# Loading q with four tokens to a partition, in two DMAs a unit, in a retention-plus-WaveMLP kernel

## The chip, the cores and the metric

The kernel runs on one core of one Trainium2 chip. The metric is device time in microseconds (us) of one execution; for the kernel before, three runs gave a median of 165.22 us (165.19 to 165.68). A core has five engines that work side by side and meet only at semaphores: TensorE (PE, with PEld for its weight loads), VectorE (DVE), ScalarE (ACT), GpSimd (POOL) and SyncE (SP). SP and ACT start DMAs from queues of their own (SPq, ACTq); POOL starts the few DMAs that change the type on the way.

## The reference

```python
state = gamma * state + k[t] outer v[t]          # per batch and head, 768 tokens, D = 64
y[t]  = scale * (q[t] @ state)                   # 4 batches, 8 heads
x     = heads of y side by side                  # (4, 768, 512)
theta = x @ w_theta
y     = w_tok_r @ (x*cos(theta)) + w_tok_i @ (x*sin(theta))     # over tokens
u     = x + y
out   = u + max(u @ w_ch, 0)
```

The first half is linear attention with one decay per head; the second mixes tokens and channels. The token mixing needs all tokens of a batch, so the second half of a batch follows its first half.

## The kernel before

The attention is cut into 24 units: 4 batches x 3 blocks of 256 tokens x 2 groups of 4 heads. A unit n loads its q, k and v (`Lq.n`, `Lk.n`, `Lv.n`, lines 154 to 170), each one DMA of 256 KB: partition p gets the tokens 2p and 2p+1 of four heads, so each DMA is 512 rows of 512 bytes. The raw q and k share a pool of 16 buffers (`kqf`), v has 9 (`vf`).

The unit's raw k is cast to bf16 (`ck`, line 295), its q is cast (`cq`) or multiplied with a decay table `qsc` (`cqs`, line 302), its v multiplied with a table `vsc` (`cv`, line 308). TensorE transposes k and q (`Tk`, `Tq`, line 316) into PSUM, `E.n` copies the result to `kqT` (or a DMA transpose `Dk.n` does both). `A.n` multiplies k with q within blocks of 128 tokens, `m.n` applies the causal mask, `ST.n` sums k times v into the state, `I.n` and `Y.n` make the output, which `XA`/`XB` copy out. The two blocks of 128 tokens of a unit are called c = 0 and 1; the head pairs j = 0 and 1. The second half works on 24 tiles of 128 tokens: `Hh` (theta), `CN` (sine and cosine), `z`, `M` (token mixing, the bulk of TensorE's work), `u`, `O` and `f`, and `SO` stores.

The order of everything is a list written out by hand, `ORDER` (lines 22 to 86). Each token is a step with the engine or queue that does it: `Lk.4.a` is the load of k of unit 4, started by ACT; `.s` is SP, `.v` DVE, `.p` POOL. Every engine runs its own steps strictly in the order of the list. The start of the list, its loads and the steps beside them, reads (with others left out):

```
const2 Lv.0.s const1 ... Lk.0.a const3 ... Lq.0.s Lv.1.s ... constA const4 Lq.1.a const9 Lk.1.s
... const8 ck.0.p Tk.0 ck.1.a cqs.0.v cv.0.v Tq.0 E.0.v Lq.4.a ST.0 Lk.4.a cqs.1.p Tq.1 Lq.2.s ... Lk.2.s
... Lv.2.s ... Lq.3.s ... Lk.3.s ... ck.3.p ... cqs.3.p Tq.3 Lv.3.s ... ck.4.p Lv.4.s Lk.5.s Lq.5.s Lv.5.s
Lq.6.s Lk.6.s Lv.6.s Lq.7.s E.3.a ...
```

Three more things set when a load starts. First, SP's and ACT's DMAs take eight semaphores in turn, in the order of the program and across both queues (`DMAHW0` to `DMAHW7` in the list of instructions); a DMA waits, on the engine that starts it, until the DMA before it on the same semaphore has landed. So a DMA waits for the eighth one before it, on whichever queue that is. Second, a buffer must be free. Third, the queue is in order: what stands behind a waiting DMA waits too.

Constants are made at the start. `const2` (lines 203 to 219) has POOL write token numbers `posn` and the eight logarithms `lg`, and DVE multiply them to `arg`; `const1` has DVE write `zero`, with which TensorE does filler products `Z` (line 278) while it has nothing else; `const3` has ACT make `qsc` and `vsc` from `arg`; `const5` is the causal mask, `constA` (line 221) POOL's `pos` and `lgp`, from which ACT makes the table `qx` in eight steps (`const9` and `const8`, line 233).

Of the kernel before, what the change touches and what calls it, by code (L numbers as in the profile page):

```python
# [15 lines left out]
FT = mybir.dt.float32  # L16
BF = mybir.dt.bfloat16
AF = mybir.ActivationFunctionType
# [70 lines left out]
def _bcast_last(ap: bass.AP, n: int) -> bass.AP:  # L89
    return bass.AP(tensor=ap.tensor, offset=ap.offset, ap=list(ap.ap) + [[0, n]])  # L90


def _bcast_mid(ap: bass.AP, n: int) -> bass.AP:
    pat = list(ap.ap)
    return bass.AP(tensor=ap.tensor, offset=ap.offset,
                   ap=[pat[0], [0, n]] + pat[1:])
# [3 lines left out]
def kernel(  # L100
# [13 lines left out]
    nc = tc.nc  # L114
    B, H, S, D = q.shape
    dm = H * D
    P = 128
    nT = S // P
    nD = dm // P
    nI = nT // 2  # L120
    HU = H // 2
    scale = 1.0 / math.sqrt(D)
    gammas = [1.0 - 2.0 ** (-5.0 - h) for h in range(H)]
# [3 lines left out]
    const = ctx.enter_context(tc.tile_pool(name="const", bufs=1))  # L127
    io = ctx.enter_context(tc.tile_pool(name="io", bufs=2))
    work = ctx.enter_context(tc.tile_pool(name="work", bufs=3))
# [3 lines left out]
    engines = {"p": nc.gpsimd, "v": nc.vector, "a": nc.scalar}  # L133

    def copy(e, dst, src):
        if e == "a":
            nc.scalar.copy(dst, src)  # L137
        else:
            engines[e].tensor_copy(dst, src)  # L139
# [4 lines left out]
    def unit(n):  # L144
        i, h = divmod(n, 2)
        b, i = divmod(i, nI)
        return b, i, h


    raw = {}  # L150

    queues = {"s": nc.sync, "a": nc.scalar}

    def load_unit(name, src, n, e):
        b, i, h = unit(n)
        t = io.tile([P, HU, 2, D], FT, name="vf" if name == "vf" else "kqf", bufs=9 if name == "vf" else 16)
        queues[e].dma_start(  # L157
            out=t.rearrange("p h a d -> p h (a d)"),
            in_=src[b, h * HU:(h + 1) * HU, i * 2 * P:(i + 1) * 2 * P, :].rearrange(
                "h (p a) d -> p h (a d)", a=2))  # L160
        raw[name, n] = t

    def Lk(n, e):
        load_unit("kf", k, n, e)

    def Lq(n, e):
        load_unit("qf", q, n, e)

    def Lv(n, e):
        load_unit("vf", v, n, e)  # L170
# [17 lines left out]
    K = {}  # L188
# [14 lines left out]
    def const2():  # L203
        posn = const.tile([P, nI, 2], FT, name="posn")
        nc.gpsimd.iota(posn, pattern=[[2 * P, nI], [1, 2]], base=1, channel_multiplier=2,
                       allow_small_or_imprecise_dtypes=True)
        lg = const.tile([P, H], FT, name="lg")
        for h in range(H):
            nc.gpsimd.memset(lg[:, h:h + 1], math.log(gammas[h]))
        K["lscale"] = const.tile([P, 1], FT, name="lscale")  # L210
        nc.gpsimd.memset(K["lscale"], math.log(scale))
        K["halfpi"] = const.tile([P, 1], FT, name="halfpi")
        nc.gpsimd.memset(K["halfpi"], math.pi / 2.0)
        K["zerob"] = const.tile([P, 1], FT, name="zerob")
        nc.gpsimd.memset(K["zerob"], 0.0)
        arg = const.tile([P, nI * 2, H], FT, name="arg")
        nc.vector.tensor_mul(arg, _bcast_last(posn.rearrange("p i a -> p (i a)"), H),
                             _bcast_mid(lg, nI * 2))
        K["arg"] = arg

    def constA():
        pos = big.tile([P, S], FT, name="pos", tag="z")
        nc.gpsimd.iota(pos, pattern=[[1, S]], base=1, channel_multiplier=0,
                       allow_small_or_imprecise_dtypes=True)
        K["pos"] = pos
        K["lgp"] = const.tile([P, H // 2], FT, name="lgp")
        for h in range(H):
            nc.gpsimd.memset(K["lgp"][(h % 2) * D:(h % 2 + 1) * D, h // 2:h // 2 + 1],
                             math.log(gammas[h]))
# [4 lines left out]
                                 bias=K["lscale"], scale=K["lgp"][:, x:x + 1])  # L234

    def const3():
        K["qsc"] = const.tile([P, nI, 2, H], FT, name="qsc")
        K["vsc"] = const.tile([P, nI, 2, H], FT, name="vsc")
        for t, bias, sc in ((K["qsc"], K["lscale"], 1.0), (K["vsc"], K["zerob"], -1.0)):
            nc.scalar.activation(t.rearrange("p i a h -> p (i a) h"), K["arg"], AF.Exp,  # L240
                                 bias=bias, scale=sc)
        K["qx"] = const.tile([P, H // 2, S], FT, name="qx")

# [13 lines left out]
        K["ident"] = ident  # L257

    def const5():
        mask = const.tile([P, 2, 2, D], BF, name="mask")  # L260
        nc.gpsimd.memset(mask, 1.0)
        for c in range(2):
            rows = slice(c * D, (c + 1) * D)
            for a in range(2):
                nc.gpsimd.affine_select(
                    out=mask[rows, a], in_=mask[rows, a], compare_op=ALU.is_ge, fill=0.0,
                    base=-a, pattern=[[1, 2], [2, D]], channel_multiplier=-2)
        K["mask"] = mask

    def const6(e):  # L270
# [10 lines left out]
    st = {}  # L281

    def kqb_of(n):
        if ("kqb", n) not in st:
            st["kqb", n] = work.tile([P, 2, dm], BF, name="kqb", bufs=5)
        return st["kqb", n]

    def by_token(ap):
        return ap.rearrange("p h a d -> p a h d")

    def in_blocks(ap):
        return ap.rearrange("p (a h d) -> p a h d", a=2, h=HU)

    def ck(n, e):
        copy(e, in_blocks(kqb_of(n)[:, 0]), by_token(raw["kf", n]))

    def cq(n, e):
        copy(e, in_blocks(kqb_of(n)[:, 1]), by_token(raw["qf", n]))

    def cqs(n, e):  # L300
        _, i, h = unit(n)
        engines[e].tensor_mul(in_blocks(kqb_of(n)[:, 1]), by_token(raw["qf", n]),  # L302
                              _bcast_last(K["qsc"][:, i, :, h * HU:(h + 1) * HU], D))

    def cv(n, e):
        _, i, h = unit(n)
# [16 lines left out]
        kq_half(n, 1)  # L323

    def E(n, e):
        kqT = work.tile([P, 2, 2, 2, P], BF, name="kqT", bufs=4)
        copy(e, kqT.rearrange("p w a j t -> p (w a j) t"), st["kq_ps", n])
        st["kqT", n] = kqT

    def Dk(n):  # L330
        kqT = work.tile([P, 2, 2, 2, P], BF, name="kqT", bufs=4)
        nc.sync.dma_start_transpose(
            out=kqT.rearrange("p w a j t -> p (w a j) t"),
            in_=st["kqb", n].rearrange("p w d -> p (w d)"))
        st["kqT", n] = kqT

    def A(n):
        kqT = st["kqT", n]
        at_ps = psum.tile([P, 2, 2, 2, P], FT, name="at_ps", tag="at", bufs=1)
        for j in range(2):  # L340
            for a in range(2):
                for c in range(2):
                    cols = slice(c * D, (c + 1) * D)
                    for g in range(2):
                        rows = slice(g * D, (g + 1) * D)
                        nc.tensor.matmul(at_ps[cols, g, j, a, :],  # L346
                                         kqT[rows, 0, a, j, cols],
                                         kqT[rows, 1, :, j, cols],
                                         start=(j == 0 and a == 0),
                                         stop=(j == 1 and a == 1), skip_group_check=True)  # L350
        st["at_ps", n] = at_ps
# [8 lines left out]
    def R_of(n):  # L360
        if ("R", n) not in st:
            st["R", n] = [bank("r_ps", f"R{c}") for c in range(2)]
        return st["R", n]
# [33 lines left out]
    def sbd_of(n):  # L397
        return K["sbd"][n % 2][n // 2 % 2]
# [7 lines left out]
    def I(n):  # L406
        _, i, h = unit(n)
        r = R_of(n + 1)
        for c in range(0 if i else 1, 2):
            for j in range(2):  # L410
                nc.tensor.matmul(r[c][:, j * P:(j + 1) * P], sbd_of(n)[:, c, j, :],  # L411
                                 st["kqT", n][:, 1, :, j, c * D:(c + 1) * D],
                                 start=(j == 0), stop=False, skip_group_check=True)

    def Y(n):
# [13 lines left out]
    def out_of(n, c):  # L429
        h, C = n % 2, n // 2 * 2 + c  # L430
        if ("xT", C) not in st:
            st["xT", C] = work.tile([P, 4, P], BF, name="xT", bufs=4)
        return (st["xT", C][:, 2 * h:2 * h + 2].rearrange("p j (t a) -> p j t a", a=2),
                st["R", n + 1][c][:, :2 * P].rearrange("p (j a t) -> p j t a", j=2, a=2))

    def XB(n, c, e):
        copy(e, *out_of(n, c))

    def XA(n, c):
        _, i, h = unit(n)  # L440
        nc.vector.tensor_mul(
            *out_of(n, c),
            K["qx"][:, 2 * h:2 * h + 2, (2 * i + c) * P:(2 * i + c + 1) * P].rearrange(
                "p j (t a) -> p j t a", a=2))

    def x_of(C):
        b, c = divmod(C, nT)
# [199 lines left out]
```

## Time and profile before

| | |
|---|---|
| median of three runs | 165.22 us |
| span of the profiled execution, first to last instruction | 163.6 us |
| around that span, against the median | 1.6 us |
| instructions | 4928 |
| PE, DVE, ACT, POOL busy | 155.2, 114.0, 78.9, 74.3 us |
| DMA packets | 69062, 34.93 MB |
| granted TensorE clock | 1.000 |

The span is cut into what each engine did; "busy" is time in which an instruction of the engine ran. Busy PE time counts pipelined products from end to end, so a PE that is 95% busy is not one at its peak, but a stretch in which it is busy all through has no wait of note. The DMA share is the time of packets, summed over 16 DMA engines and divided by 16 and the stretch; packets overlap, so it goes above 1. A row of the timeline gives start, duration, engine, line and operation; what stands in brackets is how long the engine idled before and what released it.

### The profile page before, as it was taken

The numbers are of one execution on the slowest core, as the hardware profiler recorded it, in microseconds if no ns is written. First come the engines' busy times: TensorE is split into PE (matmuls) and PEld (weight loads), VectorE is DVE, ScalarE is ACT, GpSimd is POOL, SyncE is SP. The second block draws the span as 40 slices with busy tenths as digits, with TensorE's granted clock in tenths as the row PEclk, the third lists the DMA queues.
The fourth block names the chain that finished last, engine by engine and source line by source line (L and its number), as shares of the span: only waits on it lengthen the run. The fifth ranks groups of instructions, "written<-read, shape, count | busy, mean of one in ns | idle before, by whom it ended". The sixth has DMA issues, their size and how long they took to land.

```text
span 163.6 us, 4928 instructions
## 1 busy us (share of the span) xinstructions
PE 155.2 (95%) x2034; PEld 87.2 (53%) x2034; DVE 114.0 (70%) x215; ACT 78.9 (48%) x140; POOL 74.3 (45%) x107
## 2 busy tenths in 40 slices
PE   5996889999999999999999999999999999999992
PEld 1453655656666655654554565554545554444561
DVE  3388687887994895984879894887867760345372
ACT  4976697974658255773343726732341616000020
POOL 7557389075034552730227599950469204600000
PEclk9999999999999999999999999999999999999999
DMA  3999999999999999999999999999897548515546
GB/s 115 297 290 255 268 283 236 275 220 286 220 162 232 223 291 139 338 203 270 324 263 198 134 268 221 242 193 298 125 245 136 103 92 227 160 64 128 129 164 224
DMA packets 69062, 34.93 MB, mean 214 GB/s; under 512 B 26416, under 2 KB 66096, under 8 KB 69040
## 3 DMA queue, kind: packets, MB, share of 16 engines
q1 hardware_dynamic: 56032, 23.73, 69.4%
q10 hardware_dynamic: 10320, 7.47, 17.7%
q0 software_dynamic: 2688, 3.41, 12.1%
q8 instruction: 16, 0.26, 0.7%
q14 instruction: 6, 0.05, 0.1%
HBM read 25.69 MB, written 6.29 MB: 196 GB/s over the span
## 4 chain that ended last, share of the span: by engine, by line
PE 76%; DMA 8%; ACT 5%; POOL 3%; issue 2%; SPq 2%; DVE 1%; POOLq 0%; ACTq 0%
PE y_ps L509 36%; PE o_ps L536 11%; PE th_ps L469 10%; DMA kqf<-in_k_dram 8%; PE r_ps L423 3%; ACT qx L233 3%; PE w_ps L491 3%; PE at_ps L346 3%; PE r_ps L411 2%; PE kq_ps L316 2%; SPq L157 2%; PE y_ps L561 2%; ACT cs L476 1%; PE x_ps L455 1%; PE r_ps L373 1%
## 5 line engine op out<-in xcount | busy, mean ns | idle before, releaser
L509 PE MATMUL y_ps<-z,wtr 128*128 128x512 bf16 x138 | 52.4, 380 | 0.0
L509 PE MATMUL y_ps<-z,wti 128*128 128x512 bf16 x138 | 52.3, 379 | 0.0
L483 POOL TENSOR_TENSOR z<-cs,x_sb 128x1024 bf16<-128x1024 bf16 x12 | 25.5, 2136 | 17.9 <-ACT cs L476 10.0
L355 DVE TENSOR_TENSOR at<-at_ps,mask 128x1024 bf16<-128x1024 f32 x24 | 29.2, 1216 | 0.2
L469 PE MATMUL th_ps<-wth,xT 128*128 128x512 bf16 x96 | 24.5, 379 | 0.5 <-ACT cs L476 0.4
L516 DVE TENSOR_TENSOR u<-y_ps,x_sb 128x512 bf16<-128x512 f32 x23 | 15.8, 688 | 12.7 <-PE y_ps L509 12.6
L542 DVE SCALAR_TENSOR_TENSOR ot<-o_ps,u 128x512 f32<-128x512 f32 x22 | 15.1, 688 | 12.5 <-PE o_ps L536 12.4
L308 POOL TENSOR_TENSOR vb<-vf,vsc 128x512 bf16<-128x512 f32 x15 | 15.6, 1041 | 17.3 <-DMA vf<-in_v_dram 16.9
L476 ACT ACTIVATE cs<-th_ps,zerob 128x512 bf16<-128x512 f32 x24 | 16.4, 685 | 13.3 <-PE th_ps L469 8.8
L536 PE MATMUL o_ps<-wch,uT 128*128 128x512 bf16 x88 | 22.6, 379 | 0.0
L476 ACT ACTIVATE cs<-th_ps,halfpi 128x512 bf16<-128x512 f32 x24 | 16.3, 686 | 11.5 <-issue 5.4
L509 PEld LDWEIGHTS <-wtr 128*128 128x128 bf16 x138 | 13.5, 98 | 12.7
L509 PEld LDWEIGHTS <-wti 128*128 128x128 bf16 x138 | 13.5, 98 | 12.0 <-issue 0.2
L139 POOL CAST sbd<-s 64x256 bf16<-64x256 f32 (+1 forms) x21 | 10.1, 481 | 20.8 <-DVE s L391 17.7
L137 ACT COPY kqT<-kq_ps 128x1024 bf16<-128x1024 bf16 x12 | 12.1, 1012 | 11.9 <-PE kq_ps L316 11.9
L469 PEld LDWEIGHTS <-xT 128*128 128x128 bf16 x96 | 8.8, 98 | 8.7 <-issue 0.5
L137 ACT CAST kqb<-kqf 128x512 bf16<-128x512 f32 x16 | 9.6, 620 | 6.9 <-DMA kqf<-in_k_dram 6.3
L536 PEld LDWEIGHTS <-uT 128*128 128x128 bf16 x88 | 8.1, 98 | 8.3
L278 PE MATMUL zz<-zero 128*128 128x512 bf16 x30 | 10.3, 476 | 1.9 <-DVE zero L192 1.9
L423 PE MATMUL r_ps<-at,vb 64*64 64x128 bf16 x384 | 9.9, 221 | 1.6 <-DVE at L355 1.6
L316 PE MATMUL kq_ps<-ident,kqb 128*128 128x128 bf16 x120 | 11.2, 220 | 0.3 <-POOL kqb L302 0.3
L139 POOL CAST kqb<-kqf 128x512 bf16<-128x512 f32 x12 | 7.2, 612 | 8.5 <-DMA kqf<-in_k_dram 8.4
(80 smaller groups left out, 208.7 us busy)
## 6 DMA issues: line engine op xcount, KB each, us to landing
vf<-in_v_dram SPq DMA_DIRECT2D x20, 256.0 KB, 5.9
kqf<-in_k_dram SPq DMA_DIRECT2D x19, 256.0 KB, 5.3
kqf<-in_q_dram SPq DMA_DIRECT2D x17, 256.0 KB, 5.8
out_dram<-ot ACTq DMA_DIRECT2D x12, 256.0 KB, 2.7
out_dram<-ot SPq DMA_DIRECT2D x11, 256.0 KB, 2.9
kqf<-in_q_dram ACTq DMA_DIRECT2D x7, 256.0 KB, 5.2
kqf<-in_k_dram ACTq DMA_DIRECT2D x5, 256.0 KB, 6.6
vf<-in_v_dram ACTq DMA_DIRECT2D x4, 256.0 KB, 5.8
```

What stands on the lines that cost most here:

```text
L137: nc.scalar.copy(dst, src)
L139: engines[e].tensor_copy(dst, src)
L308: engines[e].tensor_mul(in_blocks(vb), by_token(raw["vf", n]), _bcast_last(K["vsc"][:, i, :, h * HU:(h + 1) * HU], D))
L355: nc.vector.tensor_mul(at.rearrange("p g j a t -> p (g j) (a t)"), st["at_ps", n].rearrange("p g j a t -> p (g j) (a t)"), _bcast_mid(K["m ...
L423: nc.tensor.matmul(st["R", n + 1][c][g * D:(g + 1) * D, j * P:(j + 1) * P], st["vb", n][rows, lo:lo + D], st["at", n][rows, g, j, a, :], s ...
L469: nc.tensor.matmul(th_ps, st["xT", C][:, j, :], K["wth"][:, j, :], start=(j == 0), stop=(j == 3))
L476: nc.scalar.activation(st["cs", C][:, w, :], st["th_ps", C], AF.Sin, bias=K["zerob" if w else "halfpi"], scale=1.0)
L483: engines[e].tensor_mul(st["z", b][:, c], st["cs", C], _bcast_mid(x_of(C), 2))
L509: nc.tensor.matmul(st["y", t], K["wT"][r][:, s0, t0 * P:(t0 + 1) * P], st["z", b][:, s0, r, :], start=(done == 0 and r == 0), stop=(done = ...
L516: nc.vector.tensor_add(st["u", t], st["y", t], st["x", b][:, t0, :])
L536: nc.tensor.matmul(o_ps, st["uT", t][:, j, :], K["wch"][:, j, :], start=(j == 0), stop=(j == nD - 1))
L542: nc.vector.scalar_tensor_tensor(st["ot", t], st["o", t], 0.0, st["u", t], ALU.max, ALU.add)
```

## The change

Only the load of q and what depends on its layout is touched; `ORDER` is the same. A unit's q now comes in two DMAs, j = 0 and 1, each for two heads: partition j*64 + p gets the tokens 4p to 4p+3 of the heads 2j and 2j+1. A DMA writes 64 partitions with 2 rows of 1024 bytes each, 128 KB. As k and v stay as they were, q's tokens now come in another order than k's, and the tables for q and the views that read it follow:

```diff
     def Lq(n, e):
-        load_unit("qf", q, n, e)
+        b, i, h = unit(n)
+        t = io.tile([P, 2, 4, D], FT, name="kqf", bufs=16)
+        for j in range(2):
+            h0 = h * HU + 2 * j
+            queues[e].dma_start(
+                out=t[j * D:(j + 1) * D].rearrange("p g a d -> p g (a d)"),
+                in_=q[b, h0:h0 + 2, i * 2 * P:(i + 1) * 2 * P, :].rearrange(
+                    "g (p a) d -> p g (a d)", a=4))
+        raw["qf", n] = t
...
     def const2():
...
+        posq = const.tile([P, nI, 4], FT, name="posq")
+        lgq = const.tile([P, H // 2], FT, name="lgq")
+        for j in range(2):
+            rows = slice(j * D, (j + 1) * D)
+            nc.gpsimd.iota(posq[rows], pattern=[[2 * P, nI], [1, 4]], base=1,
+                           channel_multiplier=4, allow_small_or_imprecise_dtypes=True)
+            for x in range(H // 2):
+                head = x // 2 * HU + 2 * j + x % 2
+                nc.gpsimd.memset(lgq[rows, x:x + 1], math.log(gammas[head]))
         lg = const.tile([P, H], FT, name="lg")
...
         K["arg"] = arg
+        argq = const.tile([P, nI * 4, H // 2], FT, name="argq")
+        nc.vector.tensor_mul(argq, _bcast_last(posq.rearrange("p i a -> p (i a)"), H // 2),
+                             _bcast_mid(lgq, nI * 4))
+        K["argq"] = argq
...
-        mask = const.tile([P, 2, 2, D], BF, name="mask")
+        mask = const.tile([P, 2, 4, D // 2], BF, name="mask")
...
-                    base=-a, pattern=[[1, 2], [2, D]], channel_multiplier=-2)
+                    base=-a, pattern=[[1, 4], [4, D // 2]], channel_multiplier=-2)
...
-        copy(e, in_blocks(kqb_of(n)[:, 1]), by_token(raw["qf", n]))
+        copy(e, in_blocks(kqb_of(n)[:, 1], 4), by_token(raw["qf", n]))
...
+    def qT(n, rows, j, c):
+        lo = j * D + c * (D // 2)
+        return st["kqT", n][rows, 1, :, lo:lo + D // 2]
...
-                                         kqT[rows, 0, a, j, cols],
-                                         kqT[rows, 1, :, j, cols],
+                                         kqT[rows, 0, 2 * a + j, cols],
+                                         qT(n, rows, j, c),
...
-                                 st["kqT", n][:, 1, :, j, c * D:(c + 1) * D],
+                                 qT(n, slice(0, P), j, c),
...
-        return (st["xT", C][:, 2 * h:2 * h + 2].rearrange("p j (t a) -> p j t a", a=2),
-                st["R", n + 1][c][:, :2 * P].rearrange("p (j a t) -> p j t a", j=2, a=2))
+        return (st["xT", C][:, 2 * h:2 * h + 2].rearrange("p j (t a) -> p j t a", a=4),
+                st["R", n + 1][c][:, :2 * P].rearrange("p (j a t) -> p j t a", j=2, a=4))
```

`const3` takes `argq` for `qsc`; `XA` and `cqs` follow with a = 4. All products, copies and scalings of a unit keep their number and their sizes.

More of the change, by code (lines that the diff above doesn't have):

```diff
@@ L236, in const3 @@
     def const3():
-        K["qsc"] = const.tile([P, nI, 2, H], FT, name="qsc")
+        K["qsc"] = const.tile([P, nI, 4, H // 2], FT, name="qsc")
         K["vsc"] = const.tile([P, nI, 2, H], FT, name="vsc")
-        for t, bias, sc in ((K["qsc"], K["lscale"], 1.0), (K["vsc"], K["zerob"], -1.0)):
-            nc.scalar.activation(t.rearrange("p i a h -> p (i a) h"), K["arg"], AF.Exp,
+        for t, arg, bias, sc in ((K["qsc"], K["argq"], K["lscale"], 1.0),
+                                 (K["vsc"], K["arg"], K["zerob"], -1.0)):
+            nc.scalar.activation(t.rearrange("p i a h -> p (i a) h"), arg, AF.Exp,
                                  bias=bias, scale=sc)
@@ L289, in by_token, with in_blocks @@
         return ap.rearrange("p h a d -> p a h d")
-    def in_blocks(ap):
-        return ap.rearrange("p (a h d) -> p a h d", a=2, h=HU)
+    def in_blocks(ap, a=2):
+        return ap.rearrange("p (a h d) -> p a h d", a=a, d=D)
     def ck(n, e):
@@ L297, in cq @@
     def cq(n, e):
-        copy(e, in_blocks(kqb_of(n)[:, 1]), by_token(raw["qf", n]))
+        copy(e, in_blocks(kqb_of(n)[:, 1], 4), by_token(raw["qf", n]))
     def cqs(n, e):
         _, i, h = unit(n)
-        engines[e].tensor_mul(in_blocks(kqb_of(n)[:, 1]), by_token(raw["qf", n]),
-                              _bcast_last(K["qsc"][:, i, :, h * HU:(h + 1) * HU], D))
+        engines[e].tensor_mul(in_blocks(kqb_of(n)[:, 1], 4), by_token(raw["qf", n]),
+                              _bcast_last(K["qsc"][:, i, :, 2 * h:2 * h + 2], D))
     def cv(n, e):
@@ L325, in E @@
     def E(n, e):
-        kqT = work.tile([P, 2, 2, 2, P], BF, name="kqT", bufs=4)
-        copy(e, kqT.rearrange("p w a j t -> p (w a j) t"), st["kq_ps", n])
+        kqT = work.tile([P, 2, 4, P], BF, name="kqT", bufs=4)
+        copy(e, kqT.rearrange("p w x t -> p (w x) t"), st["kq_ps", n])
         st["kqT", n] = kqT
     def Dk(n):
-        kqT = work.tile([P, 2, 2, 2, P], BF, name="kqT", bufs=4)
+        kqT = work.tile([P, 2, 4, P], BF, name="kqT", bufs=4)
         nc.sync.dma_start_transpose(
-            out=kqT.rearrange("p w a j t -> p (w a j) t"),
+            out=kqT.rearrange("p w x t -> p (w x) t"),
             in_=st["kqb", n].rearrange("p w d -> p (w d)"))
         st["kqT", n] = kqT
+    def qT(n, rows, j, c):
+        lo = j * D + c * (D // 2)
+        return st["kqT", n][rows, 1, :, lo:lo + D // 2]
     def A(n):
@@ L443, in XA @@
             K["qx"][:, 2 * h:2 * h + 2, (2 * i + c) * P:(2 * i + c + 1) * P].rearrange(
-                "p j (t a) -> p j t a", a=2))
+                "p j (t a) -> p j t a", a=4))
     def x_of(C):
```

## The prediction

> **What bounds the kernel now.** I read the page first, then the table by stretches of time, then the chain of work that ended last, and last the queues of SP, ACT and POOL over the first 30 us.
>
> ```profile
> span 163.6 us, 4928 instructions
> PE 155.2 (95%) x2034; PEld 87.2 (53%) x2034; DVE 114.0 (70%) x215; ACT 78.9 (48%) x140; POOL 74.3 (45%) x107
> ...
> 5.00:10.00 5.00, 4.73 (x58) 2.45 (x57) 3.24 (x7) 4.46 (x8) 3.00 (x6) 1.00 1.22 290
> 10.00:15.00 5.00, 3.89 (x102) 2.43 (x100) 3.85 (x8) 4.03 (x7) 3.65 (x5) 1.00 1.23 290
> 30.00:40.00 10.00, 9.99 (x129) 6.28 (x132) 8.28 (x18) 6.76 (x12) 5.55 (x6) 1.00 1.16 258
> 140.00:150.00 10.00, 10.00 (x51) 4.71 (x49) 3.93 (x7) 0.00 (x0) 1.54 (x1) 1.00 0.48 144
> ```
>
> The stretch rows give busy PE, PEld, DVE, ACT, POOL, then the clock, the DMA share and GB/s. From 30 us to 150 us PE never waits (9.99 and 10.00 of 10 us): there the time is PE's work, and no load can shorten it. Before that PE is short of input (3.89 of 5 us), and DMA runs flat out: 290 GB/s, so 262144 bytes / 290 GB/s = 0.90 us for each load of 256 KB. So the end is the moment at which PE gets its unbroken work, plus a fixed amount. The chain shows that moment:
>
> ```profile
> 3.95 4.90 ACT qx L233 x8
> 8.85 0.43 ACT kqb L137
> 9.32 6.61 DMA kqf<-in_k_dram
> 15.94 0.37 SPq L157
> 16.36 0.51 SPq L157
> 16.91 0.51 SPq L157
> 17.46 1.81 SPq L157
> 19.31 5.96 DMA kqf<-in_k_dram
> 25.37 1.14 ACT kqb L137 x2
> 26.51 1.17 ACT cs L476 x2
> 27.72 1.02 PE th_ps L469 x4
> ```
>
> ACT makes `qx` in eight steps, casts k of unit 1 (`ck.1.a`), and only then starts `Lq.4.a` and `Lk.4.a` (9.32). `Lk.4` lands at 15.93, and at 15.94 SP starts `Lk.5`: that is the wait for the eighth DMA before. Behind it in SP's queue come `Lq.5`, `Lv.5`, `Lq.6`, `Lk.6` (19.31), which lands at 25.3, lets `ck.6.a` run, and at 27.72 `Hh.3` starts the unbroken stretch. The semaphores, not the bytes alone, tie SP's queue to ACT's.
>
> **The change part by part.**
>
> *The start on POOL and DVE.* `const2` gets two iotas and eight memsets of 64x1 more, ahead of all that POOL does, and DVE one product more.
>
> ```profile
> 0.91 0.15 POOL L205 IOTA posn<- 128x6 f32 x1 [0.39 <-POOLq L631]
> 1.02 0.32 POOL L209 MEMSET lg<- 128x1 f32 x8
> 3.68 1.07 POOL L228 MEMSET lgp<- 64x1 f32 x8
> 1.38 0.21 DVE L217 TENSOR_TENSOR arg<-posn,lg 128x48 f32<-128x48 f32 x1 [1.38 <-POOL lscale L211]
> 1.59 0.27 DVE L192 MEMSET zero<- 128x256 uint32 x1
> 8.85 0.43 ACTq L157 DMA_DIRECT2D kqf<-in_q_dram  x1
> ```
>
> Two iotas are 2 x 0.15 = 0.30 us. Eight memsets took 0.32 us as `lg` and 1.07 us as `lgp`, so the addition is 0.62 to 1.37; I take 1.2, since `lgp` has the same 64x1 form. On DVE the product adds 0.21, so `zero`, the fillers behind it and the table load that ACT starts after `argq` come 1.4 later. `qx` needs `lgp` and moves from 3.95 to 5.15; with it `ck.1.a` from 8.85 to 10.05, and the loads behind it: `Lq.4` half 0 at 10.05, half 1 at 10.5, `Lk.4` at 10.95 (0.43 each to start, and a gap).
>
> *The semaphores.* Every q now takes two of the eight. Which DMA waits for which follows from the lists of instructions; SP's list of the changed kernel reads, from the third load of q on:
>
> ```
> 9  L173 DMACopy kqf<-in_q_dram 64x2x256 [waits DMAHW7_49]    Lq.3, half 0
> 10 L173 DMACopy kqf<-in_q_dram 64x2x256 [waits DMAHW0_49]    Lq.3, half 1
> 11 L159 DMACopy kqf<-in_k_dram 128x4x128 [waits DMAHW1_49]   Lk.3
> 12 L159 DMACopy vf<-in_v_dram 128x4x128 [waits DMAHW2_49]    Lv.3
> ```
>
> The DMAs before these on semaphores 0, 1 and 2 are ACT's `Lq.4` half 0, half 1 and `Lk.4`. In the kernel before, SP meets these three only at `Lv.4` and `Lk.5`; unit 3 waited for loads of unit 1, long landed, and SP started its k at 8.38. Now SP stands before unit 3 until ACT is through with `qx` and its load has landed.
>
> ```profile
> 8.38 0.51 SPq L157 DMA_DIRECT2D kqf<-in_k_dram  x1
> DMA to landing us min/median/max: 3.7/5.4/12.7
> kqf<-in_q_dram SPq DMA_DIRECT2D x1, 256.0 KB, 4.5
> kqf<-in_k_dram SPq DMA_DIRECT2D x1, 256.0 KB, 5.0
> 13.54 0.62 POOL L139 CAST kqb<-kqf 128x512 bf16<-128x512 f32 x1
> 14.12 1.05 POOL L302 TENSOR_TENSOR kqb<-kqf,qsc 128x512 bf16<-128x512 f32 x1
> 16.35 0.39 PE L316 MATMUL kq_ps<-ident,kqb 128*128 128x128 bf16 x4
> 24.11 0.40 ACT L137 CAST sbd<-s 64x256 bf16<-64x256 f32 x1
> 25.37 1.14 ACT L137 CAST kqb<-kqf 128x512 bf16<-128x512 f32 x2 [0.85 <-DMA kqf<-in_k_dram]
> ```
>
> The shortest landing of a q or k load is 3.7 us, the two loads of unit 3 took 4.5 and 5.0 in a full pipe. While SP waits, the pipe runs empty, so I take 3.7 for `Lq.4`: half 0 lands at 10.05 + 3.7 = 13.75, half 1 at 14.2, `Lk.4` at 14.7. SP starts `Lq.3` half 1 at 13.75, `Lk.3` at 14.25, `Lv.3` at 14.95. With 4.0 us (3.7 to 5.0) `Lk.3` lands at 18.25, where it landed at 8.38 + 5.0 = 13.4. POOL casts k and scales q of unit 3 from 18.25 instead of 13.54, done at 18.25 + 0.58 + 1.05 = 19.9; PE's transposes of that q, at 16.35 before, come at 19.9, 3.55 late, and PE, in order, holds back all behind them.
>
> What is late next: the steps from there to `ck.6.a` are a chain of compute (unit 3 to 5), and ACT was free at 25.37 - 0.85 = 24.52, waiting for `Lk.6`. With 3.55 more it is free at 28.07. Is `Lk.6` there by then? It now waits for `Lv.3`: 14.95 + 5.4 = 20.35, plus the 5.96 of the chain = 26.3. It is. So `ck.6.a` starts 28.07 - 25.37 = 2.7 later, and PE's unbroken work with it. The delay of 1.4 of the fillers and of units 0 to 2 runs beside this wait and does not add. With the small ends (0.62 and 3.7 us) the same steps give 1.8; with the large ones (1.37 and 5.0 for both landings) 5.1, so I keep +1.8 to +5.1 and take +2.7, near the small end because the pipe is empty.
>
> *The packets.* A load of q has 256 packets of 1024 bytes in place of 512 of 512.
>
> ```profile
> q1 hardware_dynamic: 56032, 23.73, 69.4%
> q10 hardware_dynamic: 10320, 7.47, 17.7%
> out_dram<-ot SPq DMA_DIRECT2D x11, 256.0 KB, 2.9
> out_dram<-oh SPq DMA_DIRECT2D x1, 128.0 KB, 2.0
> ```
>
> Queue 1 spent 0.694 x 16 x 163.6 / 56032 = 32.4 ns on a packet of 424 bytes, queue 10 44.9 ns on one of 724. The line through both gives 36 ns at 512 bytes and 57 at 1024, so a q takes 16 engines 0.91 us instead of 1.15, a gain of 0.24. By `Lk.6` that is 7 x 0.24 = 1.7 us of pipe; but the path above waits for semaphores and not for the pipe, so it gains nothing there. No row shows a load into 64 partitions. At the other end each half could take as long as a whole load, 0.90 us, and a q 0.90 more; I take an unchanged 0.90 for a q.
>
> [...]
>
> *Issue slots.* SP starts 17 more DMAs, ACT 7.
>
> ```profile
> L157 SPq DMA_DIRECT2D kqf<-in_q_dram x17: 367/557/2704, 1.3 to 111.6; - x17
> L157 ACTq DMA_DIRECT2D kqf<-in_q_dram x7: 375/439/537, 1.8 to 101.2; - x7
> 38.51 0.69 DVE L308 TENSOR_TENSOR vb<-vf,vsc 128x512 bf16<-128x512 f32 x1
> vf<-in_v_dram SPq DMA_DIRECT2D x1, 256.0 KB, 13.1
> ```
>
> That is 17 x 0.56 = 9.5 us on SP and 7 x 0.44 = 3.1 on ACT. Behind them wait SP's DMA transposes and ACT's copies, which PE needs. What hides them is the lead of the loads, and it is small in one place: `Lv.7`, started at 24.45, landed 13.1 us later at 37.55, used at 38.51, a lead of 0.95. A start that all shares keeps that lead; the slots and later waits may use it up. I take 0.7 for the rest of the kernel, 0 to 3.
>
> *At nothing:* the mask, `E`, `cq`, `cqs`, `A`, `I`, `XA` and `XB` keep count and size; only strides change (four runs of 32 in place of two of 64). If strided reads cost 10%, the `at_ps` products would add 0.02 us to each of 24 units, hidden before 28 us and 0.4 in all after it.
>
> **Sum.** Span 163.6 + 2.7 + 0.7 = 167.0; with the 1.6 around it 168.6 against the median of 165.22.
>
> **Rivals.**
> *Faster, by the packets.* If SP's wait before unit 3 is short, because `Lq.4` lands early, the shorter packets bring `Lk.6` up to 1.7 us sooner; ACT can use 0.85 of it, then its own work binds: 164.4. For it: the pipe is the bound up to 28 us (290 GB/s). Against: ACT cannot start `Lq.4` before `qx` is done, and POOL's additions push that back. It decides if unit 3's k lands before 14.7 us, when 1.2 us of slack between POOL and PE would cover it.
> *Only the start shows.* Unit 3's delay is covered by fillers and by ACT's 0.85, what remains is the start: 1.4 - 0.85 = 0.55, so 165.8. For it: PE runs fillers between 9 and 17 us. Against: PE's order is fixed, and the transposes of unit 3 stand in front.
> *Half loads are slow.* With up to 1.8 us for a q, the seven of the start bring 7 x 0.9 = 6.3 us more of pipe. About half of that falls into the time in which the pipe stands still for the semaphores (an estimate: 3 us between 10 and 16 us); 3.1 remain on top of the 2.7, and 1 more from `Lv.7`'s lead: 165.2 + 2.7 + 3.1 + 1 = 172.0. For it: nothing in this trace; against it: a store of 128 KB landed in 2.0 us, one of 256 KB in 2.9, though both use all partitions. [...]
>
> **How the numbers follow.** The forecast, 168.6, 0.57; slow half loads 0.21; only the start 0.13; faster 0.09. The range takes the forecast's own ends, 1.6 + 163.6 + 1.8 = 167.0 and, with 5.1, 170.3 to 171, and reaches down to "only the start" and up to the slow half loads: 165.7 to 172.3, leaving out about 0.1 at each end. A difference of 0.3% (0.5 us) is about what a measurement of this kernel can tell from none: faster 0.09, same 0.05 (part of "only the start"), slower 0.86.
>
> **What would show it.** In the changed kernel's SP queue a wait from about 10 to 13.7 us that ends as an ACT load of q lands; the GB/s of 10 to 15 us well below 290; POOL idle before the cast of unit 3's k until about 18; `th_ps` of 27.72 at about 30.4; PE busy 10 of 10 us after that, and 69062 - 24 x 256 = 62918 packets. The forecast is wrong if unit 3 arrives before 15 us, if the 5 us rows stay at 290 GB/s while q takes longer (slow halves), or if PE has new idle time after 35 us.

## The result, and the profile after

The changed kernel takes 175.50 us (median of four runs, 174.95 to 176.75), the kernel before 165.30 us beside it: a ratio of 1.0612, with a 95% interval of 1.0565 to 1.0659. The change makes the kernel 10.2 us slower. The forecast was 3.4 us slower, with a range that ended at 172.3. The direction was right, the size was not. Some executions run in a slower state: ratios in this document leave them out, as does the median given for `a_two_whole`, and three of the four runs of `a_one` were such.

The profiled execution took 175.81 us with a span of 174.1. The page of the changed kernel, and its table by stretches of time (busy PE, PEld, DVE, ACT, POOL, then clock, DMA share, GB/s):

```profile
span 174.1 us, 4941 instructions
PE 155.1 (89%) x2006; PEld 88.0 (51%) x2034; DVE 116.1 (67%) x216; ACT 78.8 (45%) x140; POOL 75.1 (43%) x117
...
5.00:10.00 5.00, 3.90 (x38) 1.89 (x36) 3.31 (x6) 5.00 (x9) 2.86 (x11) 1.00 0.90 212
10.00:15.00 5.00, 3.92 (x85) 2.42 (x85) 3.97 (x7) 3.34 (x7) 1.92 (x3) 1.00 1.01 240
15.00:20.00 5.00, 2.36 (x58) 1.29 (x59) 3.21 (x8) 1.26 (x3) 2.73 (x4) 1.00 0.94 186
20.00:25.00 5.00, 4.54 (x78) 3.29 (x77) 1.52 (x4) 2.51 (x6) 1.36 (x4) 0.66 1.16 257
30.00:40.00 10.00, 8.32 (x161) 5.46 (x162) 7.74 (x17) 7.95 (x14) 4.32 (x5) 1.00 1.16 245
70.00:80.00 10.00, 9.06 (x153) 5.54 (x153) 7.68 (x15) 6.51 (x11) 5.49 (x5) 1.00 1.27 238
90.00:100.00 10.00, 8.83 (x120) 4.82 (x124) 7.75 (x13) 4.10 (x10) 4.67 (x8) 1.00 1.30 225
110.00:120.00 10.00, 8.20 (x107) 4.37 (x94) 7.01 (x15) 5.01 (x10) 7.28 (x9) 1.00 1.28 241
```

PE does the same work (155.1 us against 155.2) in a longer span, so all that was added is waiting. It is in two places. From 5 to 20 us the pipe (the DMA engines together) carries 212, 240 and 186 GB/s where it carried 290, 290 and 243. And after 30 us, where PE was busy 9.99 of 10 us, it now has gaps (8.32, 9.06, 8.83, 8.20) while the DMA share in these rows is 1.16 to 1.30, no lower than in the rows of before. The packets are 63302, not the 62918 of the forecast: the 24 added DMAs brought 384 packets of under 512 bytes (26800 against 26416), 16 each.

The rows of SP's and POOL's queues and of PE and ACT that answer to the start of the chain of before:

```profile
9.28 0.60 ACTq L173 DMA_DIRECT2D kqf<-in_q_dram  x1
9.57 0.60 ACT L137 CAST kqb<-kqf 128x512 bf16<-128x512 f32 x1
9.77 4.64 SPq L173 DMA_DIRECT2D kqf<-in_q_dram  x2
14.76 0.37 SPq L159 DMA_DIRECT2D kqf<-in_k_dram  x1
18.13 0.60 POOL L139 CAST kqb<-kqf 128x512 bf16<-128x512 f32 x1 [2.27 <-DMA kqf<-in_k_dram]
19.84 0.40 PE L340 MATMUL kq_ps<-ident,kqb 128*128 128x128 bf16 x4 [2.12 <-POOL kqb L326]
22.28 0.59 SPq L159 DMA_DIRECT2D kqf<-in_k_dram  x1
30.83 1.14 ACT L137 CAST kqb<-kqf 128x512 bf16<-128x512 f32 x2 [1.65 <-DMA kqf<-in_k_dram]
```

SP stands 4.64 us at the two halves of `Lq.3`, `Lk.3` starts at 14.76, POOL casts it at 18.13 (13.54 before), and PE's transposes of unit 3 start at 19.84 (16.35). Then `Lk.6` starts at 22.28 and ACT uses it at 30.83, where it used it at 25.37. The chain of work that ended last says what PE waits for after that; its shares, which were PE 76% and DMA 8% before, and its longest DMAs behind 27 us (start, us, what; `x_sb<-xT` is a DMA transpose, the others are loads):

```profile
PE 50%; DMA 27%; POOL 6%; SPq 6%; issue 6%; DVE 3%; ACT 1%; POOLq 0%; DVEq 0%; ACTq 0%
...
27.40 10.76 DMA row<-in_moe_w_tok_r_dram
50.75 7.58 DMA vf<-in_v_dram
64.76 7.15 DMA vf<-in_v_dram
77.77 5.38 DMA x_sb<-xT
87.13 4.84 DMA kqf<-in_q_dram
```

If PE's weight loads of both kernels are paired in order, which they have in common, the delay of each is a curve: 0.85 us at the start, 1.2 at 8.5 us of the time before, 3.7 at 16, 5.5 at 26, 6.1 at 33, 7.1 at 62, 8.1 from 65, 8.9 from 84, 10.5 from 103 us to the end. Some 6 us are lost up to the unbroken stretch, and 4 more behind it.

### The profile page after: what moved, and what is told of

Same layout as the page of the kernel before. It is cut to its first block, busy times and chain, and to the rows that moved or that the text cites. A ratio compares the mean times of both kernels' runs of the same rounds, so it can differ in the third digit from the quotient of the medians.

```text
span 174.1 us, 4941 instructions
## 1 busy us (share of the span) xinstructions
PE 155.1 (89%) x2006; PEld 88.0 (51%) x2034; DVE 116.1 (67%) x216; ACT 78.8 (45%) x140; POOL 75.1 (43%) x117
## 2 busy tenths in 40 slices
DMA packets 63302, 34.93 MB, mean 201 GB/s; under 512 B 26800, under 2 KB 60336, under 8 KB 63280
## 4 chain that ended last, share of the span: by engine, by line
PE 50%; DMA 27%; POOL 6%; SPq 6%; issue 6%; DVE 3%; ACT 1%; POOLq 0%; DVEq 0%; ACTq 0%
PE y_ps L537 23%; DMA vf<-in_v_dram 11%; PE o_ps L564 8%; DMA row<-in_moe_w_tok_r_dram 6%; PE th_ps L497 6%; SPq L173 4%; DMA kqf<-in_k_dram 3%; DMA x_sb<-xT 3%; PE r_ps L451 3%; DMA kqf<-in_q_dram 3%; POOL vb L332 2%; SPq L159 2%; PE at_ps L374 2%; PE y_ps L589 2%; PE kq_ps L340 2%
## 5 line engine op out<-in xcount | busy, mean ns | idle before, releaser
L537 PE MATMUL y_ps<-z,wti 128*128 128x512 bf16 x131 | 49.6, 379 | 1.0 <-issue 1.0
L537 PE MATMUL y_ps<-z,wtr 128*128 128x512 bf16 x131 | 49.7, 379 | 0.3
L497 PE MATMUL th_ps<-wth,xT 128*128 128x512 bf16 x88 | 23.9, 379 | 0.8 <-ACT cs L504 0.4
L504 ACT ACTIVATE cs<-th_ps,halfpi 128x512 bf16<-128x512 f32 x24 | 16.3, 684 | 12.2 <-PE th_ps L497 6.2
L139 POOL CAST sbd<-s 64x256 bf16<-64x256 f32 (+1 forms) x21 | 10.2, 484 | 21.9 <-DVE s L419 18.2
L340 PEld LDWEIGHTS <-kqb 128*128 128x128 bf16 x120 | 8.2, 100 | 8.2 <-POOL kqb L326 3.8
```

The source lines that it names most:

```text
L340: nc.tensor.transpose(st["kq_ps", n][:, 4 * w + x, :], st["kqb", n][:, w, x * P:(x + 1) * P], K["ident"])
L497: nc.tensor.matmul(th_ps, st["xT", C][:, j, :], K["wth"][:, j, :], start=(j == 0), stop=(j == 3))
L504: nc.scalar.activation(st["cs", C][:, w, :], st["th_ps", C], AF.Sin, bias=K["zerob" if w else "halfpi"], scale=1.0)
L537: nc.tensor.matmul(st["y", t], K["wT"][r][:, s0, t0 * P:(t0 + 1) * P], st["z", b][:, s0, r, :], start=(done == 0 and r == 0), stop=(done = ...
```

## The experiments

The change has four parts that can be had alone: the tables at the start; two DMAs in place of one, with the semaphores they take; 64 partitions in place of 128 for each DMA; rows of 1024 in place of 512 bytes. My theory after the trace was that the semaphores cost what was forecast and that the loads into 64 partitions are slow, here and in the rest of the kernel; the rivals were that two DMAs cost alone, that long rows are bad, that the start or the clock costs.

**The parts alone, on the kernel before.** `b_two_whole` loads q in two DMAs of two heads each, over all 128 partitions; `b_two_half` in two DMAs of 64 partitions each, with the tokens where they were; both in 512-byte rows. `b_prelude` only makes the added tables, which nothing uses.

```diff
 # b_two_whole, per j                         # b_two_half, per j
+ out=t[:, 2*j:2*j + 2]                       + out=t[j*D:(j + 1)*D]
+ in_=q[b, h*HU + 2*j:h*HU + 2*j + 2,         + in_=q[b, h*HU:(h + 1)*HU,
+       i*2*P:(i + 1)*2*P, :]                 +       i*2*P + j*P:i*2*P + (j + 1)*P, :]
```

> The kernel before, with q in two DMAs of two heads each, both over all 128 partitions in 512-byte rows: twice the DMAs for q, same packets, no new tables. If the semaphores and the issue slots are the cause, SP stops before the second half of q of unit 3 as in the changed kernel, TensorE's transposes of unit 3 come about 2.5 us later than 16.35, and the time is 169 to 171 us. If the loads into 64 partitions are the cause, little happens: 165.2 to 166.5.

> The kernel before, with q in two DMAs of 128 tokens each, one for partitions 0 to 63 and one for 64 to 127, in 512-byte rows. Semaphores and slots as in the run with two whole-partition DMAs. If the semaphores are all, the same time as there, within 0.7 us. If loads into 64 partitions are slow, 3 us or more above it, and the DMA rate between 5 and 15 us falls from 290 GB/s to under 250.

> The kernel before, with the two iotas, eight memsets and the product on VectorE that the change adds at the start; nothing uses their result. Both theories: the fillers and the cast of unit 1's k start 0.6 to 1.4 us later, ScalarE's 0.85 us of waiting before unit 6 takes most of it: 165.2 to 166.2 us.

`b_two_whole` took 169.33 us (168.71 to 170.50) against 165.56 of before: 1.0238 (1.0186 to 1.0289). `b_two_half` took 176.14 (174.97 to 176.69): 1.0631 (1.0580 to 1.0682). `b_prelude` took 166.23 (166.00 to 166.83): 1.0051 (1.0028 to 1.0073). So the start alone costs 0.7 us, two DMAs cost 3.8, and the same two DMAs on half of the partitions each 6.8 more. The stretches of `b_two_whole`, then of `b_two_half`:

```profile
5.00:10.00 5.00, 3.46 (x53) 1.96 (x52) 3.31 (x6) 4.36 (x8) 2.34 (x6) 1.00 0.93 224
10.00:15.00 5.00, 3.83 (x100) 2.51 (x100) 4.01 (x7) 3.75 (x7) 2.89 (x3) 1.00 1.02 268
30.00:40.00 10.00, 9.65 (x143) 6.13 (x142) 9.19 (x20) 8.59 (x14) 5.34 (x6) 1.00 1.13 238
```

```profile
5.00:10.00 5.00, 3.27 (x32) 1.56 (x30) 2.38 (x3) 4.46 (x8) 2.08 (x4) 1.00 0.97 192
10.00:15.00 5.00, 4.78 (x81) 2.79 (x71) 3.18 (x7) 1.29 (x3) 1.34 (x2) 0.66 1.07 217
30.00:40.00 10.00, 9.49 (x162) 5.66 (x164) 6.92 (x13) 6.95 (x13) 5.63 (x6) 0.80 1.13 247
```

With the same number of DMAs, packets of the same size and a DMA share that is a little higher (0.97 against 0.93, 1.07 against 1.02), the halves move 192 and 217 GB/s where whole loads move 224 and 268. The delay of `b_two_whole` is 3.6 at 19 us and 3.4 from 32 us to the end; that of `b_two_half` is 9.8 at 24 us, 9.7 at 32 and 11.1 at the end. Up to 82 us both kernels have the same DMA on the same semaphore throughout, so these 6 us of difference come from the halves alone.

`b_two_whole` also shows what the forecast would have met without the halves. Its `Lk.6` starts at 22.38 and lands 5.75 us later, at 28.13, just as ACT comes free for it:

```profile
28.23 1.14 ACT L137 CAST kqb<-kqf 128x512 bf16<-128x512 f32 x2
```

That is `ck.6.a` 2.86 us later than before, with no wait of ACT ahead of it.

**The wait of SP taken away.** In `a_unit4_sp` the changed kernel has `Lq.4` and `Lk.4` started by SP, behind unit 3's loads, so that SP meets no load that ACT starts late. `k2_unit4_sp` does the same to `b_two_whole`, `b_unit4_sp` to the kernel before.

```diff
-... E.0.v Lq.4.a ST.0 Lk.4.a cqs.1.p ... Tk.3 Z.3 ck.4.p Lv.4.s ...
+... E.0.v ST.0 cqs.1.p ... Tk.3 Z.3 Lq.4.s Lk.4.s ck.4.p Lv.4.s ...
```

> The changed kernel, with q and k of unit 4 started by SP, behind the loads of unit 3, instead of by ScalarE ahead of unit 2. SP then meets no load of ScalarE on its semaphores before unit 3. If the wait for ScalarE is the main cost, k of unit 3 lands at 13.5 to 15 us instead of 18.3, TensorE's unbroken work starts 3 us sooner, and the time is 170 to 172 us. If the slow half loads are the main cost, less than 1.5 us is won: 174 to 175.5.

> The run with two whole-partition DMAs a unit, but q and k of unit 4 started by SP behind the loads of unit 3. If the 3.9 us of that run come from SP's wait for ScalarE's loads, the wait before unit 3 goes and the time falls to 165.5 to 167. If they come from the issue slots or other semaphore pairs, it stays at 168 to 170.

> Control: the kernel before with unit 4's q and k started by SyncE behind unit 3's loads instead of by ScalarE. The gain that this move brought in the changed kernel (170.7 instead of 175.5) is the removed wait that the change had added: here 165.0 to 166.0 us, no change. Rival, the move is a gain of its own, change or not: below 164.5 us.

`a_unit4_sp` took 170.68 us (168.86 to 171.01), 1.0278 (1.0204 to 1.0352) of the kernel before: 4.8 less than the changed kernel. `k2_unit4_sp` took 166.16 (165.79 to 166.89), 1.0045 (1.0025 to 1.0064): 3.2 less than `b_two_whole`. `b_unit4_sp` took 165.74 (165.57 to 166.24), 1.0011 (0.9994 to 1.0028): the move is worth nothing where the wait does not exist. So nearly all that two DMAs cost is SP's wait for ACT's loads; with whole loads the slots themselves (the time that a queue takes to start a DMA) and all later semaphores cost 0.7 us (0.4 to 1.1 by the interval). In the two kernels without the wait the granted clock is 1.00 in every stretch, where the changed kernel shows 0.66 from 20 to 25 us and `b_two_whole` 0.87 and 0.78 from 15 to 25, so the 4.8 and the 3.2 us hold what the fall of the clock costs as well. The pair `k2_unit4_sp` and `a_unit4_sp` shows the halves in a full pipe, without that wait (the second has its q in 1024-byte rows too); their stretches in this order:

```profile
5.00:10.00 5.00, 3.95 (x54) 2.06 (x52) 3.32 (x6) 4.38 (x8) 2.35 (x6) 1.00 1.22 291
10.00:15.00 5.00, 3.89 (x101) 2.53 (x100) 4.00 (x7) 3.77 (x7) 4.44 (x5) 1.00 1.22 290
```

```profile
5.00:10.00 5.00, 3.55 (x34) 1.64 (x32) 2.92 (x5) 4.65 (x8) 2.34 (x8) 1.00 1.15 230
10.00:15.00 5.00, 4.23 (x87) 2.65 (x89) 3.94 (x8) 3.28 (x7) 2.79 (x5) 1.00 1.20 241
```

The share is as good as the same, the rate is 241 against 290. In `k2_unit4_sp` v of unit 2 lands at 11.45 and v of unit 3 at 14.16, so q, k and v of a unit take 2.71 us, three times 0.90. In `a_unit4_sp` the same two land at 13.51 and 16.81: 3.29 us (a landing is the last of the semaphore events of a DMA). The 0.58 us more, put on q alone, make it 1.48 us in place of 0.90, an estimate from this one interval that the rates bear out (three loads of 256 KB at 241 GB/s take 3.26 us). A half load also holds its queue longer: 0.62 us in place of 0.48 (medians of the 48 in `b_two_half` and in `b_two_whole`).

**Late units alone.** `b_half_late` takes the halves of `b_two_half` for units 10 to 23 only, `b_whole_late` the loads of `b_two_whole` for the same units; the start of the kernel is that of before.

```diff
     def Lq(n, e):
+        if n < 10:
+            return load_unit("qf", q, n, e)
+        ...
```

> The kernel before with q in two DMAs over half the partitions each, for units 10 to 23 only. It shows what the later part of the kernel pays by itself. If TensorE's unbroken work hides it, 165 to 166 us. In the changed kernel TensorE's delay grew from 5.5 us at the start to 10.5, 4.1 of it after unit 10's transposes: if that comes from the late loads themselves, 168 to 170.

> As the run before it, but both DMAs of a unit over all 128 partitions. Semaphores and slots without half loads: if the late cost comes from them, within 1 us of the run with late half loads; if from the half loads, 165 to 166.5 us.

`b_half_late` took 169.20 us (168.20 to 169.60), 1.0200 (1.0161 to 1.0239); `b_whole_late` 165.98 (165.34 to 166.93), 1.0037 (1.0012 to 1.0061). Fourteen pairs of half loads late in the kernel, where PE never waited before, cost 3.2 us more than fourteen pairs of whole ones. The two profiled executions lie closer, 168.20 and 166.87, and show less than half of that. The delay of `b_half_late` grows at two places, by 1.2 us at 84 us of the time before (`b_whole_late`: 0.5) and by 0.9 at 103 us (`b_whole_late`: nothing). Its chain at the first:

```profile
77.44 4.98 DMA vf<-in_v_dram
82.44 0.61 ACTq L173
83.09 0.63 ACTq L173
83.76 0.65 ACT xT L137 x2
84.87 1.22 DVE at L365
```

ACT starts the two halves of a q here when the v that is the eighth DMA before has landed, and only behind them does it make `xT`, which PE needs. A semaphore puts ACT behind the pipe, and the pipe is late: that v took 4.98 us, and 4.04 in `b_whole_late`, where ACT waits at the same place and makes `xT` at 83.34.

At the second place ACT starts four loads of q and then makes `sbd`, which PE needs. Here are the last three of the four in `b_whole_late`, in `b_half_late` and in the changed kernel, and for the changed kernel the cast that makes `sbd`:

```profile
102.59 1.52 ACTq L172 DMA_DIRECT2D kqf<-in_q_dram  x3
103.12 2.46 ACTq L173 DMA_DIRECT2D kqf<-in_q_dram  x3
110.21 3.11 ACTq L173 DMA_DIRECT2D kqf<-in_q_dram  x3
113.36 0.30 ACT L137 CAST sbd<-s 64x128 bf16<-64x128 f32 x1 [3.03 <-DMA out_dram<-ot]
```

The half loads take ACT longer to start, and the fourth waits for a store of SP on the same semaphore; in `b_whole_late` none of the four waits. From about 80 us on the kernels with half loads have a few DMAs on other semaphores than those with whole ones, though `ORDER` is the same; why is not known. So `b_half_late` against `b_whole_late` is not the speed of the loads alone. In the changed kernel this place makes the last 1.6 us of the curve (8.9 to 10.5).

**Rows of 1024 bytes over all partitions.** `a_one` keeps the rows of 1024 bytes and loads q in one DMA: partition 2p + j has the tokens 4p to 4p+3 of the head pair j. The tables for q then differ between even and odd partitions and are made by a longer chain on POOL and DVE. `a_one2` has that chain behind the work that ACT's first loads wait for. `a_two_whole` cuts the DMA of `a_one2` in two, one for each head of the pairs, each still over all partitions.

```diff
-        for j in range(2):
-            h0 = h * HU + 2 * j
-            queues[e].dma_start(
-                out=t[j * D:(j + 1) * D].rearrange("p g a d -> p g (a d)"),
-                in_=q[b, h0:h0 + 2, ...].rearrange("g (p a) d -> p g (a d)", a=4))
+        queues[e].dma_start(                                   # a_one, a_one2
+            out=t.rearrange("p g a d -> p g (a d)"),
+            in_=q[b, h * HU:(h + 1) * HU, ...].rearrange(
+                "(j g) (p a) d -> p j g (a d)", j=2, a=4))
+        for g in range(2):                                     # a_two_whole
+            ...  out=t[:, g]  in_= the same [:, :, g]
```

> q in one DMA per unit over all 128 partitions, still with four tokens to a partition in 1024-byte rows: partition 2p+j takes head pair j, the tables and the view of q transposed follow. As many DMAs as in the kernel before, so the semaphores pair as there; half as many packets for q; no 64-partition load; some seven small instructions more at the start. If semaphores and half loads are the whole cost of the change, 165 to 167 us (the start as in the run with the added start alone, less what the longer rows give, at most 0.85 us). If 1024-byte rows themselves are bad here, above 168.

> q in one DMA a unit over all 128 partitions in rows of 1024 bytes (partition 2p+j holds four tokens of one head pair), with the tables' product placed so that the first loads of ScalarE start no later than in the kernel before. Half loads and the added semaphores are the whole cause: 165.0 to 166.5 us, granted clock of 1.00 in 15-25 us, 290 GB/s or more in 5-15 us. Rival, the 1024-byte rows themselves are slow: above 168 us, and under 260 GB/s in 5-15 us.

> The kernel with q in one DMA a unit over all partitions in rows of 1024 bytes (165.6 us), now cut into two DMAs a unit again, one for each head of the pairs, so that each still goes over all 128 partitions, in 1024-byte rows. Only the number of DMAs differs, and with it the semaphores. If the added semaphores cost by themselves what they cost with 512-byte rows (3.9 us), and the halves are a cost apart from them: 168.5 to 169.6 us, with SyncE waiting 3 us or more before unit 3's k. Rival, the semaphores cost only together with loads into 64 partitions or with the late start of ScalarE's loads: 165.5 to 166.5 us. Rival, two DMAs of 128 KB are what is slow, whatever partitions they go to: above 172 us.

`a_one` missed: one run took 167.73 us and three 172.42 to 173.16. In the profiled one, of 172.42, the longer chain made ACT's table load start at 4.63 us in place of 1.67, and ACT's first q behind it; PE waited 3.08 us for that q. That says nothing of the rows. `a_one2`, with the chain out of the way, took 165.57 us (165.39 to 166.25): 1.0003 (0.9985 to 1.0021), no change. `a_two_whole` took 169.52 (168.36 to 170.65): 1.0230 (1.0163 to 1.0296), which is what two whole DMAs cost with 512-byte rows (1.0238). The stretches of `a_one2`:

```profile
5.00:10.00 5.00, 4.52 (x54) 2.34 (x54) 3.92 (x7) 4.94 (x9) 3.24 (x9) 1.00 1.14 310
10.00:15.00 5.00, 3.89 (x102) 2.63 (x103) 3.90 (x7) 3.98 (x7) 4.27 (x5) 1.00 1.17 269
20.00:25.00 5.00, 4.15 (x76) 2.67 (x76) 4.18 (x9) 4.83 (x10) 4.00 (x7) 1.00 1.15 318
```

The longer rows are a small gain for the pipe: 310 and 318 GB/s stand where 290 and 283 were before, but 269 where 290 was; from 5 to 25 us it is 282 against 277, at a share of 1.13 against 1.20. It brings no time; that the steps behind the loads bind there is likely, and no run shows it. So neither the rows nor the layout of the tokens costs anything.

**The clock.** In the changed kernel the granted clock fell to 0.66 from 20 to 25 us, after PE had waited 2.12 us for unit 3. `a_warm` adds five pairs of filler products in front of unit 3's transposes.

> The changed kernel with five filler matmul groups more ahead of unit 3's transposes, so that TensorE does not idle while it waits for unit 3. The lowered clock of 20-25 us costs by itself: 174.3 to 175.0 us and a granted clock near 1.00 in 20-25 us. Rival, the clock falls in time in which TensorE would wait for loads anyway: 175.3 to 175.8 us, no change, with the time turning up as a longer wait for Lk.6.

It took 178.26 us (177.42 to 179.93), 1.0772 (1.0709 to 1.0836): slower than the changed kernel. POOL's queue and the wait of PE show why this is no test of the clock:

```profile
14.02 0.93 POOL L183 DMA_DIRECT2D wth<-in_moe_w_theta_dram  x1
21.72 0.60 POOL L139 CAST kqb<-kqf 128x512 bf16<-128x512 f32 x1 [6.77 <-DMA kqf<-in_k_dram]
23.39 0.60 PE L340 MATMUL kq_ps<-ident,kqb 128*128 128x128 bf16 x4 [3.28 <-POOL kqb L326]
```

The first half of ACT's `Lq.4` was started at 9.66 us in place of 9.28 and landed at 15.0 in place of 13.8, so `Lk.3` was started at 15.66, behind POOL's load of the 512 KB of `wth` at 14.02; in the changed kernel it was started just ahead of it (14.76 and 14.93). Behind `wth` it is there for POOL at 21.72 in place of 18.13. PE then waits 3.28 us all the same, and the clock falls again (0.84 from 20 to 25 us, 0.82 from 25 to 30). Why `Lq.4` landed later is not known: no instruction ahead of it differs. What the clock costs by itself stays open.

## Why the prediction was right in direction and wrong in size

The chain before, `b_prelude`, `a_unit4_sp`, after takes the change in steps: 165.56 to 166.23 for the start (0.7), to 170.68 for half loads in 1024-byte rows with their slots (4.4), to 175.50 for SP's wait (4.8). The sum of 9.9 is the measured 10.2 within its spread. The forecast had 0 for the start, 0.7 for the slots with nothing for half loads, and 2.7 for SP's wait.

- *The start.* Its steps came, at two thirds of the size: `zero` came 0.85 us later (forecast 1.4), `qx` 0.81 (1.2), `ck.1.a` 0.72 (1.2). Alone it costs 0.7 us; whether it hides behind the wait of SP in the changed kernel, as the forecast had it, no run shows, since `b_prelude` has no such wait.
- *The semaphores.* The mechanism held: SP's wait at `Lq.3`, the landing of the first half of `Lq.4` (13.8 against 13.75), the start of `Lk.3` (14.76 against 14.25), POOL's cast (18.13 against 18.25), PE's transposes of unit 3 (19.84 against 19.9). Some of this closeness is luck: ACT started `Lq.4` at 9.28, not at 10.05, and it landed after 4.5 us, not 3.7; `Lk.3` started 0.5 late and landed after 3.3 us, not 4.0. In `b_two_whole`, without halves, `ck.6.a` is 2.86 us late, where the forecast had 2.7.
- *The failed step* is the sentence on `Lk.6`, "It is there", with the term it rests on, "I take an unchanged 0.90 for a q". `Lk.6` was to be started at 20.35 and to land 5.96 later, so that compute would bind and 0.85 us of ACT's wait would absorb part. It was started at 22.28, landed 8.45 us later, and ACT still waited 1.65 us for it: the pipe binds there, and `ck.6.a` is 5.46 late where 2.7 was forecast. The halves make the difference: `b_two_whole` starts its `Lk.6` as late, at 22.38, but it lands after 5.75 us, and ACT does not wait. In a full pipe a q in halves takes 1.48 us by the estimate above.
- *The rest of the kernel*, forecast at 0.7 with 3 as the upper end, took 4 us. The lead of the loads was taken to be lost at one place only; it was lost at several (2.0 us up to 65 us, 0.8 at 84, 1.6 at 103). Half loads are behind it: `b_half_late` costs 3.2 us more than `b_whole_late`, by slower loads, longer starts on ACT and a wait for a store on a shared semaphore, whose shares stay open. Nor is it a fixed sum: `b_two_half` has the same halves and loses only 1.4 us behind 32 us. The slots of whole loads cost 0.7 us, as much as was forecast, but 0.6 us of delay is there by 8.5 us already.
- *The packets.* That shorter packet time brings nothing was right: `a_one2` has all of that gain and is at 1.0003. It could not repay the halves.
- *The rivals.* "Half loads are slow" was the right one, at 172.0 and a chance of 0.21. It came out 3.5 us low, since it gave the rest of the kernel 1 us. Its 5.8 us for the beginning are near the 6.1 measured, partly by luck: it priced the q at 0.90 us more, above the measured 0.58, and hid half of that in SP's wait. The wait and the slow loads do not hide each other: SP's wait costs 3.2 us with whole loads and 4.8 with halves. "Only the start" and "faster" are excluded.
- *The signs.* New idle time of PE after 35 us, named as a sign against the forecast, came. The sign given for slow halves, rows that stay at 290 GB/s, was wrong: slow halves show as a lower rate (241 against 290 GB/s in `a_unit4_sp`) at nearly the same share (1.20 against 1.22), and so look like SP's wait in the rate alone.

The runs give the term for a q in halves a size: 241 against 290 GB/s with whole loads of k and v in the mix, and by the estimate above 1.48 us for a q where I took 0.90. The row that I set against slow halves, stores over all partitions that land in 2.0 and 2.9 us, said nothing of loads into half of them. With no row of the trace on the point, the unchanged 0.90 was a choice and no measurement. Why loads into halves run at a lower rate no run shows.

## What to carry to other kernels

Cut a load by heads or by bytes rather than by partitions: here two DMAs over 64 partitions each made a 256 KB load take 1.48 us in place of 0.90, an estimate from landings in a pipe that loads fill, and `b_two_half` 6.8 us slower than `b_two_whole`. Where DMAs of several queues take a few semaphores in turn, each DMA more in one queue moves all others onto other partners; follow which slow queue the fast one now waits for, and move that load to the queue that would wait (4.8 us here). When a wait and slower transfers come together in a part that is bound by loads, add their costs and do not set one off against the other (here the wait cost 3.2 us with whole loads and 4.8 with loads in two DMAs).

## What was not expected of the hardware

The granted clock fell after short waits of PE. Rows of the changed kernel, in which the same two filler products take 0.60 us before the wait and 1.06 behind it:

```profile
17.12 0.60 PE L302 MATMUL zz<-zero 128*128 128x512 bf16 x2
19.84 0.40 PE L340 MATMUL kq_ps<-ident,kqb 128*128 128x128 bf16 x4 [2.12 <-POOL kqb L326]
20.67 1.06 PE L302 MATMUL zz<-zero 128*128 128x512 bf16 x2
```

The granted clock of the changed kernel was 0.50 from 20.36 to 23.77 us, 1.00 before, and 1.00 again from there to 173.9 us. A wait of PE of 1.11 us, up to 15.08, had left it at 1.00; the wait of 2.12 us came just ahead of the fall. In `a_warm` the wait of 3.28 us went with 0.84 and 0.82 in the two stretches from 20 to 30 us. The length of the wait is not all: in `b_two_half` PE waited no longer than 1.05 us from 7.3 to 12.2 us, and the clock was 0.66 from 10 to 15, but the 1.11 us that PE waited up to 17.01 went with 1.00 from 15 to 20. What brings the clock down, and what brings it back, these runs do not show.

The order of two loads on different queues, 0.2 us apart in the changed kernel, goes with most of the 3.6 us by which POOL got unit 3 later in `a_warm`: behind the 512 KB of `wth` a load of 256 KB took 6.0 us from start to landing, ahead of it 3.3. In the changed kernel the next load behind `wth`, started at 15.46, took 6.48 us. No run moves `wth` alone.
